# A chunked complex-decay attention with a soft mixture of experts on one core: two chunks' gates joined, masks and results by whole chunks, and a new order of the work

## The chip, the cores and the metric

One core of a Trainium2 chip runs the kernel. The metric is the device time of one execution in microseconds. Other cores of the chip take no part.

## The reference

Two layers follow each other. The first is a linear attention with a complex decay, over 4 batches, 8 heads, 768 steps and a head dimension of 48; the second is a soft mixture of 8 experts with 4 slots each over all 3072 tokens of width 384.

```python
mag = np.sqrt(a_re * a_re + a_im * a_im)
scale = np.minimum(mag, 0.999) / (mag + 1e-06)
for t in range(S):                       # S_re, S_im: 48 x 48 per batch and head
    new_re = ar * S_re - ai * S_im       # ar, ai: a_re, a_im times scale at step t
    new_im = ar * S_im + ai * S_re
    S_re, S_im = new_re + outer(k_t, v_t), new_im
    y_t = q_t @ S_re
logits = x @ phi                         # x: y with the heads side by side
d = softmax(logits, axis=0); c = softmax(logits, axis=1)
slot_out[e] = relu((d.T @ x)[e] @ w1[e]) @ w2[e]
out = c @ slot_out
```

## The kernel before

The sequence is cut into 12 chunks of 64 steps. A chunk j is two tiles (2j and 2j+1), each of 128 partitions: two batches of 64 steps. The decay is used in polar form, so the recurrence inside a chunk becomes products with running sums of logarithms and angles.

The work is a set of small tasks, each a Python generator that issues one step per call, and the string `ORDER` (line 295) names them one by one: a token is a task and, after a colon, its bank of PSUM. `run` (line 883) plays it, and after each token pins the instructions, so that every engine keeps this order. What follows on an engine waits for what stands in front of it there. The tasks:

- `la` loads a group of gates (a_re, a_im), `g` turns them into logarithms of magnitudes by 8 steps (`gates`, line 637), `t` takes the arctangent. A group holds the chunks that `STEPS` (line 47) names: the two tiles of chunk 0 each by itself, chunks 1, 2 and 3 each, then pairs. ScalarE has two sets of tables; `L` and `T` load the one for logarithm and exponential, or that for the angles.
- `p` (line 687) sums angles with TensorE, rounds them to whole turns (VectorE for the first two chunks, then ScalarE) and takes the rest. `v` makes sine and cosine, `e` the exponentials of the summed logarithms; `K` carries the sums into the next chunk.
- `m` multiplies k and q by the exponentials (line 766): the k half by VectorE, the q half by GpSimd. `h` (line 777) multiplies by cosine and sine: the hat, a tile of 1536 columns.
- `xk` and `xq` turn the hats on TensorE and copy the result (line 793); the copy is VectorE's for the tiles and halves of `COPY_V` (line 41: k of tiles 0 to 7, q of tiles 0 to 3), ScalarE's otherwise.
- `c` (line 803), one for each tile, makes scores and masks them; `D` adds to the state; `A` (line 834) gives the results of a chunk, copied for one tile by ScalarE and for the other by VectorE; `F` turns them (copy by ScalarE); `d` applies a decay at chunk 5.
- For each pair of chunks, `l` (line 108) makes the logits and `s` (line 135) the slots' running sums and each token's shares. `s` has the exponential's accumulator give each row's sum `z`, kept in `zrun`, and turns the shares into `ecT`. `me` and `si` merge the slots' sums and give the experts' inputs. `er` (line 271) spreads the turned shares over the experts by products with constant matrices (`C_REP`), in 12 pieces, and masks them.
- `w:` loads one of 32 tiles of expert weights (768 KB, two loads) into a buffer that an earlier task gives back: `wx` are its own, `ar`, `qkt`, `hat` and so on are those of attention. 23 of them stand in the order, each with a wait on the TensorE instruction in front of it in the order and on the third load before it; 9 follow as the first layer of the experts gives buffers back (`used`, line 973).

All loads are issued on SP's queue. After the order come the two expert layers (`hidden`, `experts`) and the mixture, whose results are stored from SP and ScalarE.

Of the kernel before, what the change touches and what calls it, by code (L numbers as in the profile page):

```python
# [11 lines left out]
F32 = mybir.dt.float32  # L12
# [3 lines left out]
ALU = mybir.AluOpType  # L16
# [22 lines left out]
BUF = dict(ar=2, ai=2, gt=1, qkt=3, vt=3, f=3, cs=3, ee=2, hat=3, hTq=3, hTk=2, scT=3, st=3, yT=3, xs=8, wx=4)  # L39
AHEAD, WAHEAD, LATE = 3, 3, 5  # L40
COPY_V = tuple((i, w) for i in range(8) for w in range(2) if i < 4 or w == 0)
PAIRS = ("p", "e", "xk", "xq", "D", "A", "F")
ROUND_V = 4
# [3 lines left out]
STEPS = [(0,), (0,), (1,), (2,), (3,)] + [(j, j + 1) for j in range(4, NCH, 2)]  # L47
# [38 lines left out]
C_REP = C_SEL + P  # L86
C_LOW = C_REP + UB * P
# [3 lines left out]
class _Moe:  # L91


    def __init__(self, nc, pool, work, tr, cst, phi_sb):
        self.nc, self.pool, self.work, self.tr = nc, pool, work, tr
        self.ident, self.sel = cst[:, C_ID:C_BU], cst[0:UR, C_SEL:C_REP]
        self.rep = [cst[0:UR, C_REP + P * j : C_REP + P * (j + 1)] for j in range(UB)]
# [4 lines left out]
        self.z = pool.tile([UR, 1], F32, name="zrun")  # L102
        self.acc = pool.tile([UR, HD], F32, name="acc")
        self.ecT = pool.tile([UR, NU, P], F32, name="ecT")
# [3 lines left out]
    def logits(self, u, yT):  # L108
# [22 lines left out]
        lc = wk.tile([P, UB, NSLOT], F32, name="lc")  # L131
        nc.vector.tensor_tensor(out=lc, in0=lt, in1=mx.broadcast_to([P, UB, NSLOT]), op=ALU.subtract)
        self.mid[u] = (ls, lc)

    def slots(self, u, xs):
        nc, wk, tr = self.nc, self.work, self.tr
        ls, lc = self.mid.pop(u)
        nm = self.nm[u]
        z = wk.tile([UR, 1], F32, name="z")
        self.act(out=ls, in_=ls, func=AF.Exp, bias=nm, accum_out=z)  # L140
# [16 lines left out]
        tp = tr([P, UR + P], "mt")  # L157
        nc.tensor.transpose(out=tp[:, 0:UR], in_=ls, identity=self.ident[0:UR, 0:UR])
# [3 lines left out]
        nc.vector.tensor_copy(out=d, in_=tp[:, 0:UR])  # L162
# [11 lines left out]
    def merge(self):  # L174
# [6 lines left out]
        mrow = wk.tile([1, UB, NSLOT], F32, name="mrow", bufs=1)  # L181
# [114 lines left out]
    L g0 g0 g0 g0 g0 g0 g0 g0 g1 g1 lv1 e0:0 g1 T t0 g1 p0:1 la2 t1 p0 L g1 g1 e0 p1:1 g1 g1 p0 la2 e0 g2 p1 p1 e1:0 g2 T v0  # L296
    g2 la3 m0 v0 la3 g2 t2 v0 p2:2 v1 v1 L g2 lq1 h0 e1 D0:1 e1 p2 g2 g2 lq2 p2 g2 K1 e2:3 g3 g3 xk0:0 la4 g3 la4 T v1 xq0:2
    w:wx g3 m1 h1 L g3 e2 xk0 g3 g3 xq0 e2 g3 g4 K2 c0:0 g4 T v2 v2 g4 m3 D1:2 m2 D0 D1 t3 e3:3 v2 g4 xq1:1 p3:2 c0 xq1 t4 L
    g4 p3 h2 h3 la5 g4 e3 xk1:0 la5 D2:1 p3 p4:2 lq3 D2 xq2:1 g4 g4 g5 m5 e3 lq4 g5 g5 p4 xk1 T v3 v3 K3 xq2 xq3:0 v3 c1:6 p4
    xq3 m4 lv2 xk2:1 v4 xk3:2 g5 e4:0 t5 xk2 h5 xk3 la6 L g5 D3:1 D3 e4 e4 c1 la6 p5:2 g5 p5 h4 g5 c2:7 A0:1 c3:6 g5 g6 A0 K4  # L300
    A0 c2 A0 c3 A0 lq5 e5:0 g6 p5 m7 xq5:3 e5 xk5:1 e5 K5 D5:2 xq5 v4 xk5 F0:0 g6 D5 p6:3 T v5 F0 v4 lv3 v5 m6 p6 A1:1 xk4:2
    xk4 xq4:0 p6 A1 g6 e6:2 c5:6 xq4 h6 c4:7 v5 lv4 c5 c4 m8 A1 xk6:0 A1 A2:3 t6 A1 v6 L g6 xk6 e6 A2 F1:0 A2 la7 e6 F1 A2 h7
    lq6 g6 xq7:1 la7 v6 D4:2 xq7 xk7:0 l0:2 A2 D4 xk7 m9 g6 l0 xq6:2 p7:3 g6 g7 w:wx lv5 D7:1 e7:0 h8 xq6 c6:4 m11 p7 D7 g7 p7
# [43 lines left out]
def _stepwise(ctx, tc, cst, phi_sb, raw, w1, w2, out):  # L347
# [125 lines left out]
    for j in range(UB):  # L473
        for _ in moe.weights(er[j], j, range(UB)):
            pass
        for u in range(UB, NU):
            for _ in moe.weights(er[u][:, j : j + 1], j, [u]):
                pass
# [38 lines left out]
def _polar(ctx, tc, cst, phi_sb, bad, aa, qk, vv, phi, w1, w2, consts, out):  # L517
# [34 lines left out]
    def two():  # L552
        return psum[:, 2 * cur["bank"] : 2 * cur["bank"] + 2]
# [595 lines left out]
```

## Time and profile before

| | us |
|---|---|
| median of 3 runs | 269.25 (268.48 to 270.42) |
| profiled execution, its own time | 265.5 |
| its span, first to last instruction | 263.7 |

Over the span TensorE was busy 80%, VectorE (DVE) 77%, ScalarE (ACT) 73% and GpSimd (POOL) 23%; 55.13 MB were moved, and the mean granted clock of TensorE was 0.949. PEld is TensorE's loading of weights, which runs beside its products. A row of a group gives line, engine, operation, result and operands with their shapes, the number of instructions, then busy time in us and the mean of one in ns, then the idle time before them and what ended it. A row of a timeline gives start and length in us; "x2" are two instructions without a gap between them.

### The profile page before, as it was taken

Reading aid. Unit: us, or ns where it says so; the run is one execution under the profiler, and the core shown is the slowest. Engines: PE = TensorE matmul, PEld = TensorE weight load, DVE = VectorE, ACT = ScalarE, POOL = GpSimd, SP = SyncE. Lnnn points to the kernel's source line nnn. Section 1 sums busy time; section 2 is a strip of 40 time slices with the busy share of each in tenths; the row PEclk is TensorE's granted clock in tenths of the full one; section 3 lists DMA queues with packets and bytes.
Section 4 is the critical chain, followed back from the end, with each engine's and each line's share of the span. In section 5 each row is a group of like instructions: output and inputs, shape, how many; then the busy total and the mean of one; then the engine's idle time right before and its main releaser. Section 6 shows DMA issues by size and latency. Waiting matters only on the chain.

```text
span 263.7 us, 12297 instructions
## 1 busy us (share of the span) xinstructions
PE 211.7 (80%) x5592; PEld 156.8 (59%) x5592; DVE 202.8 (77%) x301; ACT 192.3 (73%) x267; POOL 59.7 (23%) x39
## 2 busy tenths in 40 slices
PE   0626465568799898899999999999989998999740
PEld 0204254245578777678788779678877745268520
DVE  1277999999999999999999889998862668126330
ACT  5998999699899999989989888798743345013320
POOL 0000033463860639040460031250000030000000
PEclk9999659795999999999999999999999999999995
DMA  6763642496321691098612036838998998899994
GB/s 200 277 217 120 221 163 82 160 309 231 121 65 62 224 280 48 5 325 273 188 53 76 6 122 202 245 116 288 307 295 280 276 295 295 280 365 346 376 398 169
DMA packets 21355, 55.13 MB, mean 209 GB/s; under 512 B 2608, under 2 KB 3120, under 8 KB 21296
## 3 DMA queue, kind: packets, MB, share of 16 engines
q1 hardware_dynamic: 20432, 52.70, 60.1%
q10 hardware_dynamic: 864, 1.57, 1.6%
q8 instruction: 46, 0.75, 1.2%
q14 instruction: 13, 0.11, 0.1%
HBM read 49.53 MB, written 4.72 MB: 206 GB/s over the span
## 4 chain that ended last, share of the span: by engine, by line
PE 39%; DVE 31%; DMA 12%; ACT 8%; issue 7%; DVEq 0%; ACTq 0%; SPq 0%
DMA w<-in_w_dram 10%; PE psum L850 7%; PE psum L807 6%; PE psum L796 5%; PE psum L823 5%; DVE hat L780 4%; DVE ar L658 4%; PE psum L842 3%; DVE qkt L773 3%; DVE ar L654 2%; PE psum L676 2%; DVE ar L729 2%; DMA ar<-in_aa_dram 2%; DVE f L698 2%; DVE hTk L801 2%
## 5 line engine op out<-in xcount | busy, mean ns | idle before, releaser
L771 POOL TENSOR_TENSOR qkt<-ee,qkt 128x384 f32<-128x384 f32 x22 | 38.4, 1765 | 61.6 <-ACT ee L721 51.4
L780 DVE TENSOR_TENSOR hat<-qkt,cs 128x1536 f32<-128x1536 f32 x24 | 42.2, 1767 | 3.8 <-PE psum L823 2.1
L796 PE MATMUL psum<-cst,hat 64*96 64x64 f32 x768 | 30.8, 225 | 3.1 <-DVE st L832 1.2
L823 PE MATMUL psum<-vt,hat 64*64 64x48 f32 x1408 | 29.1, 231 | 4.7 <-DVE hTk L801 1.6
L823 PEld LDWEIGHTS psum<-vt,hat 64*64 64x64 f32 x1408 | 26.1, 145 | 9.5 <-DVE hTk L801 2.3
L807 PE MATMUL psum<-hTq,hTk 96*64 96x64 f32 x768 | 28.3, 231 | 4.0 <-DVE hTq L801 3.9
L807 PEld LDWEIGHTS psum<-hTq,hTk 96*64 96x64 f32 x768 | 25.5, 144 | 10.0 <-DVE hTq L801 4.1
L796 PEld LDWEIGHTS psum<-cst,hat 64*96 64x96 f32 x768 | 25.2, 127 | 10.5 <-issue 3.3
L648 POOL TENSOR_TENSOR ai<-ai,gt 128x768 f32<-128x768 f32 x9 | 18.7, 2094 | 56.4 <-ACT gt L642 56.4
L850 PE MATMUL psum<-st,hTq 96*64 96x48 f32 x704 | 25.5, 224 | 0.3 <-issue 0.3
L850 PEld LDWEIGHTS psum<-st,hTq 96*64 96x64 f32 x704 | 22.6, 138 | 2.7 <-issue 1.6
L801 ACT COPY hTq<-psum 96x1024 f32<-96x1024 f32 x20 | 20.0, 1007 | 3.0 <-PE psum L796 2.8
L811 DVE TENSOR_TENSOR scT<-psum,cst 128x512 f32<-128x512 f32 x24 | 16.0, 681 | 7.1 <-PE psum L807 7.1
L830 DVE TENSOR_TENSOR st<-psum,st 96x768 f32<-96x768 f32 x20 | 18.8, 945 | 0.7 <-PE psum L823 0.7
L801 ACT COPY hTk<-psum 96x1024 f32<-96x1024 f32 x16 | 16.0, 1004 | 4.2 <-PE psum L796 3.3
L676 PE MATMUL psum<-ai,cst 64*64 64x384 f32 x88 | 11.9, 602 | 8.1 <-ACT ai L662 3.6
L842 PEld LDWEIGHTS psum<-vt,scT 64*64 64x64 f32 x768 | 12.3, 135 | 4.7 <-DVE ar L729 0.9
L556 ACT ACT_TABLE_LOAD x11 | 14.1, 1283 | 0.9 <-PEq L1129 0.7
L676 PE MATMUL psum<-ar,cst 64*64 64x384 f32 x88 | 9.9, 519 | 5.8 <-DVE ar L729 4.8
L842 PE MATMUL psum<-vt,scT 64*64 64x48 f32 x768 | 13.8, 220 | 0.8 <-DVE ar L729 0.7
L256 PE MATMUL psum<-w,hz 128*32 128x128 f32 x384 | 12.6, 275 | 1.9 <-DMA w<-in_w_dram 1.7
L867 ACT COPY yT<-psum 128x768 f32<-128x768 f32 x12 | 9.6, 798 | 5.5 <-PE psum L864 5.3
(126 smaller groups left out, 405.1 us busy)
## 6 DMA issues: line engine op xcount, KB each, us to landing
w<-in_w_dram SPq DMA_DIRECT2D x64, 384.0 KB
qkt<-in_qk_dram SPq DMA_DIRECT2D x24, 384.0 KB
vt<-in_vv_dram SPq DMA_DIRECT2D x12, 384.0 KB
ar<-in_aa_dram SPq DMA_DIRECT2D x11, 384.0 KB
ai<-in_aa_dram SPq DMA_DIRECT2D x11, 384.0 KB
out_dram<-os SPq DMA_DIRECT2D x12, 256.0 KB
out_dram<-os ACTq DMA_DIRECT2D x6, 256.0 KB
cst<-in_consts_dram SPq DMA_DIRECT2D x1, 386.0 KB
```

The source lines that it names most:

```text
L648: POOL.tensor_tensor(out=i[:, z : z + 2], in0=i[:, z : z + 2], in1=t[:, z : z + 2], op=ALU.mult)
L676: PE.matmul(out=o[C * x : C * (x + 1), y], lhsT=m[r], rhs=g[r, x], start=True, stop=c == 0)
L771: POOL.tensor_tensor(out=t[:, y], in0=ee[j][:, y, w], in1=t[:, y], op=ALU.mult)
L780: DVE.tensor_tensor(out=t, in0=qkt[j][:, y].rearrange("p w (h d) -> p w h d", d=D).unsqueeze(3).broadcast_to([P, 2, H, 2, D]), in1=cs[j][: ...
L796: PE.transpose(out=tp[:, x, h], in_=hat[j, y][half(x), w, h].rearrange("p c d -> p (c d)"), identity=ident[half(x), half(x)])
L801: f(out=t, in_=tp)
L807: PE.matmul(out=sp[half(x), h], lhsT=hT[j, y, 0][:, x, h], rhs=hT[j, y, 1][:, x, h], start=True, stop=True)
L811: DVE.tensor_tensor(out=t, in0=sp, in1=mask[j % 2].unsqueeze(1).broadcast_to([P, H, C]), op=ALU.mult)
L823: PE.matmul(out=db[m : m + 64, x, D * h : D * h + D], lhsT=k_, rhs=vt[j][half(x), y, h, :], start=True, stop=True)
L830: DVE.tensor_tensor(out=t, in0=d, in1=st[j - 1][:, _batches(j, y)], op=ALU.add)
L842: PE.matmul(out=yb[half(x ^ y), y, h], lhsT=scT[j, y][half(x), h], rhs=vt[j][half(x), y, h, :], start=h == 0, stop=h == H - 1 and j == 0)
L850: PE.matmul(out=yb[half(x ^ y), y, h], lhsT=hT[j, y, 1][:, x, h], rhs=st[j - 1][:, _batch(j, y, x), h, :], start=False, stop=h == H - 1)
```

## The change

- Chunks 2 and 3 become one group of gates, as the later pairs are: 8 groups instead of 9.
- `score` takes a chunk: the products of both tiles, in two banks, and then one mask over 1024 columns. `attend` ends with one copy of 768 columns instead of two of 384.
- In the slot steps the accumulator and `zrun` go; the slots' sums are products of the slot weights with a column of ones, one column beside the 384 of `acc`. The turning of the shares goes from there too; shares are kept, and `er`, now 6 tasks, copies them spread out (ScalarE unless said otherwise), turns four 128x128 squares on TensorE and masks them. The constant matrices for spreading go: 512 columns.
- A token can name an engine after `@`. 9 of the q copies, 5 of the k copies, 5 roundings, 2 copies of results, 4 copies of turned results, 2 spreading copies and one gate square are VectorE's; the k products of chunks 1 to 11 (all 11) and one gate product of chunk 0 are GpSimd's. Otherwise a copy is ScalarE's.
- Buffers: 4 of q/k (3), 2 of cosines (3), 2 of masked scores, each for a chunk (3 for a tile), 4 of results for a chunk (8 for a tile).
- The order is a new one, of 678 tokens instead of 733. Its table loads are 19 instead of 21. Of the weights' loads, 4 are for q/k buffers (3) and 2 for cosines (3).

```diff
-BUF = dict(ar=2, ai=2, gt=1, qkt=3, vt=3, f=3, cs=3, ee=2, hat=3, hTq=3, hTk=2, scT=3, st=3, yT=3, xs=8, wx=4)
+BUF = dict(ar=2, ai=2, gt=1, qkt=4, vt=3, f=3, cs=2, ee=2, hat=3, hTq=3, hTk=2, scT=2, st=3, yT=3, xs=4, wx=4)
-STEPS = [(0,), (0,), (1,), (2,), (3,)] + [(j, j + 1) for j in range(4, NCH, 2)]
+STEPS = [(0,), (0,), (1,)] + [(j, j + 1) for j in range(2, NCH, 2)]
...
-        self.act(out=ls, in_=ls, func=AF.Exp, bias=nm, accum_out=z)
+        self.act(out=ls, in_=ls, func=AF.Exp, bias=nm)
...
-        nc.tensor.transpose(out=tp[0:UR, UR : UR + P], in_=lc.rearrange("p a s -> p (a s)"), identity=self.ident)
...
-        nc.vector.tensor_copy(out=self.ecT[:, u, :], in_=tp[0:UR, UR : UR + P])
...
-        sp = tr([UR, HD], "sip")
+        sp = tr([UR, HD + 1], "sip")
         for j in range(UB):
-            nc.tensor.matmul(out=sp[32 * j : 32 * j + 32, :], lhsT=d[:, 32 * j : 32 * j + 32], rhs=xs(j), start=True, stop=True)
+            r = slice(32 * j, 32 * j + 32)
+            nc.tensor.matmul(out=sp[r, HD : HD + 1], lhsT=d[:, r], rhs=self.ones, start=True, stop=True)
+            nc.tensor.matmul(out=sp[r, 0:HD], lhsT=d[:, r], rhs=xs(j), start=True, stop=True)
...
-    def weights(self, out, j, us):
-        ep = self.tr([P, len(us), P], "ep")
-        self.nc.tensor.matmul(out=ep, lhsT=self.rep[j], rhs=self.ecT[:, us[0] : us[-1] + 1, :], start=True, stop=True)
+    def weights(self, out, u):
+        r = self.work.tile([P, 4 * UB, 4, 8], F32, name="rep", bufs=1)
+        v = self.share[:, u].rearrange("p a (g r) -> p (a g) r", g=4).unsqueeze(2).broadcast_to([P, 4 * UB, 4, 8])
+        self.copy("A", r, v)
+        yield "er0"
+        ep = self.tr([P, UB, P], "ep")
+        for a in range(UB):
+            self.nc.tensor.transpose(out=ep[:, a], in_=r[:, 4 * a : 4 * a + 4].rearrange("p g q r -> p (g q r)"), identity=self.ident)
...
+    def copy(engine, out, in_):
+        f = DVE.tensor_copy if on(engine) == "V" else ACT.copy
+        f(out=out, in_=in_)
...
-            DVE.tensor_tensor(out=t, in0=ee[j][:, :, w], in1=t, op=ALU.mult)
+            f = POOL if on("V") == "G" else DVE
+            f.tensor_tensor(out=t, in0=ee[j][:, :, w], in1=t, op=ALU.mult)
...
-    def score(j, y):
-        sp = tr([P, H, C], "sp")
+    def score(j):
+        sp = two()[:, :, 0 : H * C].rearrange("p y (h t) -> p y h t", t=C)
...
-            xs[j, y] = buf("xs", [P, HD])
-            f = DVE.tensor_copy if y else ACT.copy
-            f(out=xs[j, y], in_=yb[:, y].rearrange("p h d -> p (h d)"))
+        yield "a3"
+        xs[j] = buf("xs", [P, 2, HD])
+        copy("A", xs[j], yb.rearrange("p y h d -> p y (h d)"))
```

The first lines of the new order:

```text
L g0 g0 g0 g0 g0 g0 g0 g0 e0:0 g1 g1 T t0 g1@G g1 t1 p0:1 la2 L g1 p0@V g1 la2 e0 p0 e0 g1 g1 g2 g2 m0 T v0 p1:1 lv1 v0 v0
p1@V g2 g2@V t2 p1 L g2 e1:0 la3 h0 g2 la3 e1 e1 p2:2 g2 p2@V g2 lq1 D0:1 xk0:3 g3 K1 g3 g3 e2:0 m1 xk0@V p2 e2 D0 e2 g3
```

## Rows read from the trace of the kernel before

**Rows 1.** Engines by stage: start:end us, length, busy time and instructions, clock, DMA.
```profile
0.00:30.00 30.00, 12.54 (x112) 5.88 (x114) 15.93 (x23) 24.35 (x41) 0.20 (x4) 0.98 0.63 210
30.00:131.00 101.00, 82.72 (x2391) 63.18 (x2390) 99.23 (x113) 95.14 (x117) 42.64 (x23) 0.90 0.52 171
131.00:222.30 91.30, 87.42 (x2605) 70.22 (x2600) 74.03 (x132) 65.47 (x97) 16.88 (x14) 1.00 0.64 202
222.30:263.70 41.40, 28.98 (x508) 17.52 (x508) 13.62 (x37) 7.38 (x14) 0.00 (x0) 0.92 0.88 318
```

**Rows 2.** The chain that ended last, from 222 us: start, length, what.
```profile
222.25 3.38 PE psum L235 x29
...
243.99 7.32 DMA w<-in_w_dram
```

**Rows 3.** SP's timeline: the last run of weight loads.
```profile
176.31 68.01 SPq L568 DMA_DIRECT2D w<-in_w_dram  x54
```

**Rows 4.** Waits of SP's queue, 160 to 252 us: total, times, longest.
```profile
SPq L568 <- DMA w<-in_w_dram: 43.0, 46, 2.5
```

**Rows 5.** Groups of instructions by form: VectorE.
```profile
L780 DVE TENSOR_TENSOR hat<-qkt,cs 128x1536 f32<-128x1536 f32 x24 | 42.2, 1767 | 3.8 <-PE psum L823 2.1 <-ACT cs L710 1.4
...
L811 DVE TENSOR_TENSOR scT<-psum,cst 128x512 f32<-128x512 f32 x24 | 16.0, 681 | 7.1 <-PE psum L807 7.1
...
L773 DVE TENSOR_TENSOR qkt<-ee,qkt 128x768 f32<-128x768 f32 x11 | 13.4, 1216 | 0.0
...
L801 DVE COPY hTk<-psum 96x1024 f32<-96x1024 f32 x8 | 9.7, 1209 | 0.0
...
L654 DVE SCALAR_TENSOR_TENSOR ar<-ar,gt 128x1536 f32<-128x1536 f32 x4 | 7.1, 1769 | 0.0
...
L856 DVE COPY xs<-psum 128x384 f32<-128x384 f32 x12 | 6.6, 552 | 3.0 <-PE psum L850 2.8
...
L654 DVE SCALAR_TENSOR_TENSOR ar<-ar,gt 128x768 f32<-128x768 f32 x3 | 3.7, 1217 | 0.0
...
L694 DVE TENSOR_SCALAR f<-psum 128x768 f32<-128x768 f32 x1 | 1.0, 958 | 0.8 <-PE psum L682 0.8
```

**Rows 6.** Timelines of GpSimd and of VectorE, single instructions.
```profile
37.19 1.92 POOL L648 TENSOR_TENSOR ai<-ai,gt 128x768 f32<-128x768 f32 x1 [36.75 <-ACT gt L642]
...
63.89 6.19 POOL L771 TENSOR_TENSOR qkt<-ee,qkt 128x384 f32<-128x384 f32 x2 [6.70 <-ACT ee L721]
...
37.35 2.58 DVE L773 TENSOR_TENSOR qkt<-ee,qkt 128x768 f32<-128x768 f32 x1
...
77.40 0.94 DVE L773 TENSOR_TENSOR qkt<-ee,qkt 128x768 f32<-128x768 f32 x1
...
130.95 1.75 DVE L780 TENSOR_TENSOR hat<-qkt,cs 128x1536 f32<-128x1536 f32 x1
```

**Rows 7.** Groups of instructions by form: ScalarE.
```profile
L801 ACT COPY hTq<-psum 96x1024 f32<-96x1024 f32 x20 | 20.0, 1007 | 3.0 <-PE psum L796 2.8
...
L556 ACT ACT_TABLE_LOAD x11 | 14.1, 1283 | 0.9 <-PEq L1129 0.7
...
L867 ACT COPY yT<-psum 128x768 f32<-128x768 f32 x12 | 9.6, 798 | 5.5 <-PE psum L864 5.3
...
L652 ACT ACTIVATE gt<-gt 128x1536 f32<-128x1536 f32 x4 | 5.9, 1485 | 0.0
...
L652 ACT ACTIVATE gt<-gt 128x768 f32<-128x768 f32 x3 | 2.5, 842 | 0.0
```

**Rows 8.** Groups of instructions by form: TensorE.
```profile
L274 PE MATMUL psum<-ecT,cst 128*128 128x512 f32 x8 | 4.4, 631 | 0.0
...
L274 PE MATMUL psum<-ecT,cst 128*128 128x128 f32 x16 | 3.3, 311 | 0.2 <-DVE er L269 0.2
...
L119 PE MATMUL psum<-cst,ls 128*128 128x128 f32 x6 | 1.9, 310 | 0.0
...
L167 PEld LDWEIGHTS psum<-xs,d 128*32 128x32 f32 x48 | 1.1, 108 | 0.3
```

More of the change, by code (lines that the diff above doesn't have):

```diff
@@ L101, in __init__ @@
         self.nm, self.mid = {}, {}
-        self.z = pool.tile([UR, 1], F32, name="zrun")
-        self.acc = pool.tile([UR, HD], F32, name="acc")
-        self.ecT = pool.tile([UR, NU, P], F32, name="ecT")
+        self.ones = cst[:, C_ONE : C_ONE + 1]
+        self.acc = pool.tile([UR, HD + 1], F32, name="acc")
+        self.z = self.acc[:, HD : HD + 1]
+        self.copy = lambda engine, out, in_: nc.scalar.copy(out=out, in_=in_)
+        self.share = pool.tile([P, NU, UB, NSLOT], F32, name="share")
         self.wz = pool.tile([UR, 2], F32, name="wz")
@@ L300 @@
[L300 to L303, printed above, removed]
@@ L472, in _stepwise @@
     er = [cp.tile([P, UB, P], F32R, name=f"er{n}") for n in range(NER)]
-    for j in range(UB):
-        for _ in moe.weights(er[j], j, range(UB)):
-            pass
-        for u in range(UB, NU):
-            for _ in moe.weights(er[u][:, j : j + 1], j, [u]):
-                pass
+    for u in range(NU):
+        for _ in moe.weights(er[u], u):
+            pass
     for x in range(NX):
@@ L561, in _polar @@
     moe = _Moe(nc, cp, ys, tr, cst, phi_sb)
+    moe.copy = copy
     ga, gt, qkt, vt = {}, {}, {}, {}
@@ L799, in xpose @@
         hT[j, y, w] = t
-        f = DVE.tensor_copy if (2 * j + y, w) in COPY_V else ACT.copy
-        f(out=t, in_=tp)
-    def score(j, y):
-        sp = tr([P, H, C], "sp")
-        for h in range(H):
-            for x in range(2):
-                PE.matmul(out=sp[half(x), h], lhsT=hT[j, y, 0][:, x, h], rhs=hT[j, y, 1][:, x, h], start=True, stop=True)
-        yield "c1"
-        t = buf("scT", [P, H, C])
-        scT[j, y] = t
-        DVE.tensor_tensor(out=t, in0=sp, in1=mask[j % 2].unsqueeze(1).broadcast_to([P, H, C]), op=ALU.mult)
+        copy("A", t, tp)
+    def score(j):
+        sp = two()[:, :, 0 : H * C].rearrange("p y (h t) -> p y h t", t=C)
+        for y in range(2):
+            for h in range(H):
+                for x in range(2):
+                    PE.matmul(out=sp[half(x), y, h], lhsT=hT[j, y, 0][:, x, h], rhs=hT[j, y, 1][:, x, h], start=True, stop=True)
+            yield f"c{y + 1}"
+        scT[j] = buf("scT", [P, 2, H, C])
+        DVE.tensor_tensor(
+            out=scT[j].rearrange("p y h t -> p (y h) t"),
+            in0=sp.rearrange("p y h t -> p (y h) t"),
+            in1=mask[j % 2].unsqueeze(1).broadcast_to([P, 2 * H, C]),
+            op=ALU.mult,
+        )
     st, yT, xs = {}, {}, {}
@@ L842, in attend @@
                     PE.matmul(
-                        out=yb[half(x ^ y), y, h], lhsT=scT[j, y][half(x), h], rhs=vt[j][half(x), y, h, :], start=h == 0, stop=h == H - 1 and j == 0
+                        out=yb[half(x ^ y), y, h], lhsT=scT[j][half(x), y, h], rhs=vt[j][half(x), y, h, :], start=h == 0, stop=h == H - 1 and j == 0
                     )
         for y in range(2):
-            yield f"a{2 * y + 1}"
+            yield f"a{y + 1}"
             if j:
@@ L948, in zeros @@
     def zeros():
-        late["zs"] = [buf("xs", [P, 3, 4, 32], name=f"zs{hi}") for hi in range(2)]
+        zs = buf("xs", [P, 2, 3, 4, 32], name="zs")
+        late["zs"] = [zs[:, hi] for hi in range(2)]
         late["hz"] = [buf("hTq", [P, 8, 4, 32], name=f"hz{hi}") for hi in range(2)]
@@ L955, in zeros @@
             POOL.memset(t, 0.0)
-    for j in range(UB):
-        at(f"er{j}", lambda j=j: moe.weights(er_tile(j), j, range(UB)))
-    for u in range(UB, NU):
-        for j in range(UB):
-            at(f"er{UB + UB * (u - UB) + j}", lambda u=u, j=j: moe.weights(er_tile(u)[:, j : j + 1], j, [u]))
+    for u in range(NU):
+        at(f"er{u}", lambda u=u: moe.weights(er_tile(u), u))
     at("ze", zeros)
```

115 lines of the change are left out of this document (54 added, 61 removed).

## Prediction

> **What bounds the kernel now.** I read first the busy time of each engine in stages that I cut myself [rows 1]: the table shows whether one engine is full in a stage, and which. Four stages come out. Up to 30 us nothing is full: the gates of chunk 0 go through ScalarE, VectorE and TensorE by turns. From 30 to 131 us VectorE is busy 99.2 of 101 us and ScalarE 95.1; TensorE has 82.7. The two vector engines bound this stage together, so only work taken from both shortens it. From 131 to 222.3 us TensorE is busy 87.4 of 91.3 us, VectorE 74.0 and ScalarE 65.5: TensorE bounds it, and what VectorE saves here is worth little. From 222.3 us the expert layers run, ending at 263.7.
>
> Then the chain that ended last [rows 2]: TensorE starts the first expert layer at 222.25, and the last piece of expert weights lands at 243.99 + 7.32 = 251.3; 12.4 us of small work and stores follow. SP's queue [rows 3] has 54 half loads of weights in one run from 176.31 for 68 us, and its waits [rows 4] say what holds it: in 46 of them, 43.0 us, it is the earlier weight load. So from 176 us the weights come as fast as the transfers go, and the end follows from when this stream can start; but its buffers are those that attention gives back, so the start follows attention. TensorE is itself busy 29.0 us from 222.3 on [rows 1], about the 29 us to the last landing: neither the stream nor attention alone could be moved by more than some 2 us without the other.
>
> **The change part by part.** Rows are means over a group unless I give a start time. I count what each order has done when tile 13 gets its hat (VectorE, at 130.95 us before [rows 6]), the end of the second stage. The counts are from the two order strings, the durations from the rows.
>
> VectorE up to there [rows 5]. The k products of chunks 1 to 6 go to GpSimd: 6 x 1.216 = 7.3 us off by the mean, 6 x 0.94 = 5.6 by one that ran undisturbed [rows 6]; I take 5.6, since the disturbance is counted apart below. Turned copies of q and k: 12 before, 8 after, 4 x 1.209 = 4.8 off. Masks: 12 x 0.681 = 8.2 become 6 of 1024 columns; the nearest row of that length from PSUM is the turned copy, 6 x 1.209 = 7.3, so 0.9 off. Results: 5 x 0.552 = 2.8 become 2 of 768 columns at 0.958, 0.9 off. Two roundings and two copies of yT come over from ScalarE, 4 x 0.958 = 3.8 on. Gates: two groups of 768 columns become one of 1536. Of the two long operations each, 4 x 1.217 go and 2 x 1.769 come, 1.3 off; a product of 768 is added and one of 384 leaves (0.4 on), and one square comes over (1.0 on): 0.1 on. What is merely later in the new order (a carry of a phase, a decay) is about 1 off. Sum: -5.6 - 4.8 - 0.9 - 0.9 + 3.8 + 0.1 - 1 = -9.3 us.
>
> ScalarE up to there [rows 7]. Table loads, 17 to 13: 4 x 1.283 = 5.1 off (over the whole kernel only two go; the others come later, where ScalarE has time). Gates: 12 x 0.842 become 6 x 1.485, 1.2 off, the square 0.8, two accumulator reads 0.4. Two roundings and two copies of yT, at 0.798, 3.2 off. Turned copies, 12 to 17: 5 x 1.007 = 5.0 on. The results, five half ones against three whole ones, about equal. One wave's exponential and rounding stand later in the order, 1.5 off. Sum -7.2 us.
>
> GpSimd [rows 6] gets 11 k products of 768 columns, some 7 of them in this stage. Its operation of that size took 1.92 us at 37.19; it is busy 42.6 of 101 us [rows 1], so there is room for 7 x 1.92 = 13.4 more, and its queue holds nothing but products, gates and, near the end, four clears. But where it works beside VectorE both slow down: the product that VectorE began at 37.35, inside that operation, took 2.58 us, the one at 77.40 took 0.94. That is 1.64 more; for 7 products the bounds are 0 and 11.5 us on VectorE. I take 2, near the low end: the product, whose mean of 1.216 against 0.94 shows it disturbed, is the one that leaves, and the hat, with a mean of 1.767 us for twice the columns [rows 5], shows little. So VectorE has about 7 us less and ScalarE 7.2 less. Both were 94 to 98% full; I take 6.5 us off this stage.
>
> The Trainium skill, SBUF — State Buffer, sections "SBUF: two separate sides" and "Who interferes with whom", speaks against this part: the port pair that GpSimd and VectorE share is an exclusive lock, and a VectorE instruction with two SBUF inputs blocks against a GpSimd instruction that reads SBUF for its whole length. The pair at 37 us [rows 6] agrees: VectorE's product ends 0.82 us after GpSimd's, as if it had begun only then. Elsewhere it is GpSimd that waits: its two halves at 63.89 took 6.19 us. By the rule the gain of this stage could be given back; that is the last case of the third rival.
>
> The head: the second load of constants shrinks by four matrices of 64 KB, and a load of v (384 KB) moves in SP's queue behind that of chunk 1's gates. At the 210 GB/s of the first stage [rows 1] this lets the gates come 262/210 = 1.2 us and 1.9 us sooner, at most 3.1 us together, and worth nothing where ScalarE is busy with chunk 0 until then, as it is for 24.35 of these 30 us. I take 0. The v of chunk 1 is needed only by its state products, some 20 us on.
>
> TensorE after tile 13 [rows 8]. Six turns of shares leave the slot steps, 6 x 0.310 = 1.9 off. The products that spread the shares, 4.4 + 3.3 = 7.7 us, become 24 turns: at most 24 x 0.310 = 7.4, and less when they follow each other; I take 5.5, 2.2 off. The slots' sums add 24 products of one column, two passes each: 48 weight loads x 0.108 = 5.2 us if none hides behind the products of 384 columns beside them, nothing if all do; 2.6. Sum -1.5, bounds +3 and -5. The sums for VectorE and ScalarE that go (slots' z, the accumulator read, the copies of turned shares) lie in stages or queues with room, and so do four new ScalarE copies of 512 columns; if the last shares were late, TensorE would wait for them before the slot inputs, a risk of about 1 us each for the last two. The scores' mask now starts after both tiles' products, so the first tile's result waits for the second's 32 products; that is hidden as long as other TensorE work stands before the results need it, which the order provides, and costs up to 1 us a chunk where not.
>
> The tail: counting TensorE work that is left, the first weight load into a gate buffer is issued about 10 us of it sooner, the fifth some 2 us sooner, and after the last q/k buffer (there are four now, the cosines give back one less) 11 gated tiles are to come where 12 were before, with 2 us less work left. One tile is 68 us / 27 = 2.5 us of stream. So the stream keeps its distance from the expert layers to within 1 us, and what attention saves is passed on.
>
> Total: 6.5 + 1.5 = 8.0 us. The profiled execution took 265.5 us, 3.75 under the median of the runs shown, 269.25. Against its own time 265.5 - 8.0 = 257.5; against the median 261.2.
>
> **The rivals.** First, the stream doesn't follow. If the weights' stream starts no earlier in time than at 176, because the wait on TensorE's place in the order holds the first q/k buffers back, the last piece still lands near 251, and only the 2 us of TensorE's waits there go: 267 to 269. For it: rows 3 and 4 show the stream as the last to end; against it: every load stands at the same or an earlier place of the work.
>
> Second, more than the sum. The merged gates spare waits of one engine for another in the first 80 us, and a denser TensorE would do stage three sooner: with VectorE's 9.3 us in full, TensorE's lower bound of 5 and 1 us of the head, -15: 254. Against it: ScalarE has only 7 to give.
>
> Third, ending on the other side: GpSimd decides when hats start. Each hat needs the k product of its chunk, and with two products per chunk GpSimd has 2 x 1.92 = 3.8 us to do undisturbed, and more where it is blocked: the two halves at 63.89 took 6.19 us [rows 6]. If k products take 3.5 us instead of VectorE's 0.94 and all 11 lie on the path, that is 28 us; with half of them covered, 14, less the 8: 275. It decides from the point where the product, once the chunk's exponentials are done, takes longer than VectorE's other work before the hat, which in the new order, summed with these durations, is 2 to 9 us. For it: the 6.19 us. Against it: GpSimd was idle for more than half of the second stage and four fifths of the third, so it starts at once. With blocking of VectorE alone, the 11 x 1.92 = 21 us more of GpSimd meet operations with two SBUF inputs (hats 42.2, long gate operations 7.1, of 202.8 us) for a quarter to a third of their time: some 6 us are given back and the time is 267, within 1%.
>
> **How the numbers follow.** Forecast (256 to 266) 0.60; more than the sum (250 to 256) 0.12; the stream or the blocking takes the gain (266.5 to 272) 0.16; GpSimd decides (over 272) 0.12. A difference of 1%, 2.7 us, is about what a measurement of this kernel can tell from none: faster 0.72, same 0.16, slower 0.12. The range 253 to 271 leaves out the lower half of the second case and the slow one, 0.18 with some of the third; the likeliest case's own range is 256 to 266.
>
> **What would show it.** Right: table loads 19, VectorE's product rows down to those of chunk 0, 22 products with GpSimd plus 11 wide ones; VectorE some 190 us busy and ScalarE 183; tile 13's hat at about 124.5, the first expert product at about 214, the last weights at about 243. Wrong: the hat of tile 13 not earlier than 128 with TensorE or VectorE waiting for GpSimd's products (GpSimd the releaser in the waits); or the expert layer earlier but the last weights still at 250.

## The result, and the profile after

| | before | changed |
|---|---|---|
| median of 20 runs each, us | 268.50 (265.15 to 273.63) | 264.36 (261.12 to 269.02) |
| profiled execution, its own time (span), us | 265.5 (263.7) | 264.75 (263.0) |
| ratio, 95% interval | | 0.9863 [0.9824, 0.9901] |

The change makes the kernel faster by 4.1 us in the medians, half of the 8.0 forecast. The ratio is taken over the faster executions of each kernel, so it lies a little nearer to 1 than the ratio of the medians (0.985). The two profiled executions show only 0.7 us of the gain: that of before lies 3.0 us under its median, that of the changed kernel 0.4 above. So I read single traces for where time sits, and take sizes from medians and from several traces together.

The page's busy times of the changed kernel's engines over its span, and TensorE's granted clock in 40 slices:

```profile
PE 208.5 (79%) x5634; PEld 156.6 (60%) x5634; DVE 197.9 (75%) x260; ACT 185.1 (70%) x237; POOL 73.9 (28%) x50
...
PEclk9986667999799999996899999999999999999975
```

Table loads are 19 (10 and 9), as in the diff. ScalarE at 185.1 us is near the 183 forecast. VectorE at 197.9 is not: 190 were expected. GpSimd has 73.9 us. The windows by stage, as in [rows 1] (columns: PE, PEld, DVE, ACT and POOL busy, granted clock, DMA share, GB/s):

```profile
0.00:30.00 30.00, 11.50 (x112) 5.46 (x112) 16.59 (x22) 25.13 (x38) 2.80 (x6) 0.85 0.62 201
30.00:131.00 101.00, 84.62 (x2435) 65.12 (x2435) 95.38 (x94) 90.56 (x103) 46.71 (x30) 0.89 0.57 182
131.00:219.80 88.80, 82.68 (x2595) 68.30 (x2588) 71.12 (x111) 61.78 (x84) 24.38 (x16) 1.00 0.61 191
219.80:263.00 43.20, 29.69 (x508) 17.73 (x508) 14.79 (x37) 7.58 (x15) 0.00 (x0) 0.88 0.86 312
```

In the second stage VectorE still works 95.4 of 101 us, ScalarE 90.6, and that stage ends nearly as before: tile 13's hat stands at 130.10 us, where it stood at 130.95 [rows 6]; 124.5 was forecast. The first expert product comes at 219.77 instead of 222.25 [rows 2], and the last stage has become 1.8 us longer.

Part of why VectorE is no emptier is in its groups by form. The mask of 1024 columns (L816) is as long as assumed (1216 ns), but of the two long gate operations (L658, L662) the first, which took 1769 ns [rows 5, there L654], now takes 2401 (2010 and 2180 in two later traces), and the second 1910:

```profile
L786 DVE TENSOR_TENSOR hat<-qkt,cs 128x1536 f32<-128x1536 f32 x24 | 43.4, 1817 | 0.0
...
L816 DVE TENSOR_TENSOR scT<-psum,cst 128x1024 f32<-128x1024 f32 x12 | 14.6, 1216 | 7.0 <-PE psum L813 7.0
...
L658 DVE SCALAR_TENSOR_TENSOR ar<-ar,gt 128x1536 f32<-128x1536 f32 x5 | 12.0, 2401 | 0.1
...
L662 DVE SCALAR_TENSOR_TENSOR ar<-ar,gt 128x1536 f32<-128x1536 f32 x5 | 9.6, 1910 | 0.0
```

The timelines of the changed kernel show when. Rows of VectorE, GpSimd and TensorE (start, length; in brackets the idle time before and what ended it):

```profile
113.91 3.40 DVE L658 SCALAR_TENSOR_TENSOR ar<-ar,gt 128x1536 f32<-128x1536 f32 x1
117.23 0.94 DVE L702 SCALAR_TENSOR_TENSOR f<-f,psum 128x768 f32<-128x768 f32 x1
...
121.49 2.56 DVE L662 SCALAR_TENSOR_TENSOR ar<-ar,gt 128x1536 f32<-128x1536 f32 x1
...
113.87 1.82 POOL L779 TENSOR_TENSOR qkt<-ee,qkt 128x768 f32<-128x768 f32 x1
116.68 2.31 POOL L779 TENSOR_TENSOR qkt<-ee,qkt 128x768 f32<-128x768 f32 x1 [0.99 <-ACT ee L728]
118.95 3.48 POOL L776 TENSOR_TENSOR qkt<-ee,qkt 128x384 f32<-128x384 f32 x2
...
118.23 0.65 PE L802 MATMUL psum<-cst,hat 64*96 64x64 f32 x16 [1.32 <-DVE f L702]
...
124.24 3.17 PE L813 MATMUL psum<-hTq,hTk 96*64 96x64 f32 x64
```

GpSimd begins a k product at 113.87, VectorE its gate operation 0.04 us later. GpSimd ends at 115.69; VectorE ends at 117.31, 1.62 us after that, about one undisturbed length (1.75): the times fit an operation that stood still until GpSimd was through. The rounded angles (L702), queued behind, come late, and TensorE waits 1.32 us for them. Between 120 and 125 us its granted clock is 0.50, its 1.2 GHz level, and 64 products take 3.17 us; that the wait brought the clock down is not shown. At 121.49 VectorE is held up again, beside the second of two q products.

This is what the Trainium skill says (SBUF — State Buffer, section "Who interferes with whom"): a VectorE instruction with two SBUF inputs and a GpSimd instruction that reads SBUF need one shared port pair, and the later one waits for the whole of the other. The trace agrees (3.40 us = 1.78 + 1.62). The rounding at 117.23, with one input from PSUM, ran its undisturbed 0.94 us inside GpSimd's next product (116.68 to 118.99), as that section says too.

The last stage, from the chain that ended last; SP's last run of loads; and, in TensorE's timeline, the last products that waited for weights:

```profile
219.77 9.65 PE psum L227 x88
...
232.28 4.72 DMA w<-in_w_dram
...
237.02 6.52 DMA w<-in_w_dram
...
243.60 7.32 DMA out_dram<-os
```

```profile
182.34 60.09 SPq L570 DMA_DIRECT2D w<-in_w_dram  x46
```

```profile
250.32 0.63 PE L248 MATMUL psum<-w,hz 128*32 128x128 f32 x12 [0.74 <-DMA w<-in_w_dram]
```

After 12.5 us of the first expert layer the chain is transfers. The weights' last run begins at 182.34 (176.31 in [rows 3], but with eight halves more in it) and its issuing ends at 242.4, where [rows 3] end at 244.3. The last weights land at 250.3, where they landed at 251.3 before [rows 2]; about 243 was forecast. So the stream gained 1 to 2 us. In two later traces of the changed kernel the chain has no weight transfer in this stage, so this reading holds for one trace.

### The profile page after: what moved, and what is told of

The parts are those of the page before. It is cut to its first block, busy times and chain, and to the rows that moved or that the text cites. A ratio compares the mean times of both kernels' runs of the same rounds, so it can differ in the third digit from the quotient of the medians.

```text
span 263.0 us, 12332 instructions
## 1 busy us (share of the span) xinstructions
PE 208.5 (79%) x5634; PEld 156.6 (60%) x5634; DVE 197.9 (75%) x260; ACT 185.1 (70%) x237; POOL 73.9 (28%) x50
## 4 chain that ended last, share of the span: by engine, by line
PE 45%; DVE 20%; ACT 16%; DMA 9%; issue 7%; ACTq 0%; DVEq 0%; SPq 0%
PE psum L813 7%; PE psum L802 6%; PE psum L860 6%; PE psum L833 6%; DMA w<-in_w_dram 4%; DVE hat L786 4%; PE psum L227 4%; DVE ar L658 4%; PE psum L852 3%; PE psum L680 3%; DMA out_dram<-os 3%; DMA ar<-in_aa_dram 2%; PE psum L873 2%; ACT gt L644 2%; ACT L560 2%
## 5 line engine op out<-in xcount | busy, mean ns | idle before, releaser
L776 POOL TENSOR_TENSOR qkt<-ee,qkt 128x384 f32<-128x384 f32 x22 | 32.9, 1515 | 29.7 <-issue 18.5
L779 POOL TENSOR_TENSOR qkt<-ee,qkt 128x768 f32<-128x768 f32 x11 | 23.3, 2121 | 38.4 <-ACT ee L728 19.8
L833 PE MATMUL psum<-vt,hat 64*64 64x48 f32 x1408 | 27.9, 233 | 4.4 <-DVE hat L786 1.8
L833 PEld LDWEIGHTS psum<-vt,hat 64*64 64x64 f32 x1408 | 25.5, 147 | 7.7 <-DVE hat L786 2.0
L649 POOL TENSOR_TENSOR ai<-ai,gt 128x768 f32<-128x768 f32 (+1 forms) x9 | 15.4, 1727 | 34.4 <-ACT gt L644 24.2
L551 ACT COPY hTk<-psum 96x1024 f32<-96x1024 f32 x19 | 18.9, 1006 | 3.6 <-PE psum L802 3.6
L816 DVE TENSOR_TENSOR scT<-psum,cst 128x1024 f32<-128x1024 f32 x12 | 14.6, 1216 | 7.0 <-PE psum L813 7.0
L551 ACT COPY hTq<-psum 96x1024 f32<-96x1024 f32 x15 | 15.0, 1005 | 5.7 <-PE psum L860 3.2
L852 PE MATMUL psum<-vt,scT 64*64 64x48 f32 x768 | 15.0, 221 | 2.2 <-issue 2.2
L658 DVE SCALAR_TENSOR_TENSOR ar<-ar,gt 128x1536 f32<-128x1536 f32 (+2 forms) x8 | 14.1, 1760 | 3.0 <-ACT gt L656 2.9
L551 ACT COPY xs<-psum 128x768 f32<-128x768 f32 x10 | 8.0, 799 | 10.3 <-PE psum L860 6.9
```

The source lines that it names most:

```text
L551: f(out=out, in_=in_)
L658: DVE.scalar_tensor_tensor(out=r, in0=r, scalar=2.0, in1=t, op0=ALU.mult, op1=ALU.add)
L776: f.tensor_tensor(out=t[:, y], in0=ee[j][:, y, w], in1=t[:, y], op=ALU.mult)
L779: f.tensor_tensor(out=t, in0=ee[j][:, :, w], in1=t, op=ALU.mult)
L833: PE.matmul(out=db[m : m + 64, x, D * h : D * h + D], lhsT=k_, rhs=vt[j][half(x), y, h, :], start=True, stop=True)
L852: PE.matmul(out=yb[half(x ^ y), y, h], lhsT=scT[j][half(x), y, h], rhs=vt[j][half(x), y, h, :], start=h == 0, stop=h == H - 1 and j == 0)
```

## The experiments

The theory after reading the two traces: the work that left VectorE did leave, but GpSimd's k products hold VectorE up by almost as much as they relieve it. The rivals: the stage is no longer VectorE's but a chain's through the hand-written order; the gain is there but the stream of weights doesn't pass it on. Each kernel was measured beside the kernel before, and the ratios are to that.

**The changed kernel once more.**

> The changed kernel as it is, once more, as the base of this group and for a second trace. Both theories: ratio to the kernel before 0.980 to 0.992; tile 13's hat between 127 and 132 us and the first expert product between 217 and 221 us, as in the first trace. If the second trace has them 3 us or more elsewhere, single traces of this kernel don't carry differences of that size.

Measured: 265.67 us, ratio 0.9919 [0.9847, 0.9991]; tile 13's hat at 129.51, but the first expert product at 225.58, 5.8 us later than in the first trace and outside the range expected, with a slower clock in the slices before it. The execution profiled took 268.39 us, 2.7 above the median. The second stage repeats from trace to trace; the third doesn't, to some 6 us.

**The k products back on VectorE** (11 tokens lose their `@G`):

```
-    m4@G D3:3 ... m6@G ... m22@G
+    m4 D3:3 ... m6 ... m22
```

> The changed kernel with the 11 products of k back on VectorE, nothing else moved. Theory 'given back' (GpSimd's products block VectorE's instructions with two SBUF operands for as long as VectorE gains): within 1.5 us of the changed kernel, ratio to before 0.981 to 0.992; VectorE's stretched gate and hat operations fall back to 1.75 us. Rival 'the move carries the gain': 4 to 8 us slower than the changed kernel, ratio 1.00 to 1.015.

Measured: 266.46 us, 0.998 [0.9938, 1.0021], hat 13 at 129.87. The gate operations are back at their length, and the seven products of this stage cost 7.9 us on VectorE. Groups by form up to 129.87 us:

```profile
L779 DVE TENSOR_TENSOR qkt<-ee,qkt 128x768 f32<-128x768 f32 x7 | 7.9, 1132 | 0.0
...
L658 DVE SCALAR_TENSOR_TENSOR ar<-ar,gt 128x1536 f32<-128x1536 f32 x4 | 7.0, 1749 | 0.1
```

So the stage takes as long with these 7.9 us on VectorE. The ratios differ by 0.6% (0.998 against 0.992) and the medians by 0.8 us; the kernel before differs from itself by 0.7% in the last run below, so no gain of the move is shown. Why the stage is no longer, with VectorE busy 115.0 us up to the hat where the changed kernel has 112.5 in the mean, isn't settled; TensorE's granted clock up to there is 0.96, and 0.88 to 0.93 in the changed kernel's traces. In the forecast 3.6 us of the 8.0 hung on it.

**No k products** for chunks 1 to 11; this kernel leaves that factor out of the computation:

```
-            f = POOL if on("V") == "G" else DVE
-            f.tensor_tensor(out=t, in0=ee[j][:, :, w], in1=t, op=ALU.mult)
+            pass
```

> The changed kernel with the products of k by the exponentials left out for chunks 1 to 11: no engine does them. Theory 'given back': 3 to 6 us faster than the changed kernel, ratio 0.964 to 0.975, since VectorE loses some 5 us of blocking up to tile 13. Rival 'the order's own waits set this stage, GpSimd costs nothing there': within 1 us of the changed kernel, ratio 0.982 to 0.990.

Measured: 259.97 us, 0.9732 [0.9628, 0.9836], hat 13 at 124.76. With the products gone and not moved, the stage is 5.3 us shorter than the mean of the changed kernel's three traces (130.06) and the end 5.7 us earlier than in the repeat above, as the theory had it. On GpSimd the products still cost the stage those 5 us, 3.8 of them as VectorE's busy time up to the hat (108.7 us here, 112.5 in the mean of the three); how far the rest is TensorE's, whose granted clock is higher here too (0.95), isn't separated. The rows of all engines up to that hat, in the kernel before, in the repeat and here (columns as above):

```profile
0.00:130.95 130.95, 95.21 (x2494) 69.01 (x2496) 115.11 (x134) 119.44 (x157) 42.80 (x26) 0.92 0.54 180
...
0.00:129.51 129.51, 95.39 (x2495) 69.39 (x2497) 112.42 (x114) 114.52 (x139) 47.59 (x34) 0.92 0.59 189
...
0.00:124.76 124.76, 92.34 (x2502) 65.79 (x2504) 108.65 (x114) 113.92 (x139) 33.74 (x27) 0.95 0.61 194
```

**The kernel before with only its k products on GpSimd**:

```
-            DVE.tensor_tensor(out=t, in0=ee[j][:, :, w], in1=t, op=ALU.mult)
+            POOL.tensor_tensor(out=t, in0=ee[j][:, :, w], in1=t, op=ALU.mult)
```

> The kernel before with only its 11 products of k moved to GpSimd, in its own order. Theory 'given back': within 1% of the kernel before, ratio 0.992 to 1.010. Rival 'the move carries the gain': 4 us or more faster, ratio 0.970 to 0.985. A third way, hats that wait for GpSimd: slower, 1.01 to 1.03, with GpSimd the releaser of the hats.

Measured: 273.32 us, 1.015 [0.9979, 1.0321], hat 13 at 135.86. The interval holds 1, so that the kernel is slower is likely and not shown. Here two hats do wait for GpSimd, as in the third rival of the prediction; VectorE's waits from 30 to 130 us (total, times, longest):

```profile
DVE hat L780 <- POOL qkt L773: 1.9, 2, 1.4
```

In the changed kernel no such wait appears in the same view: no hat is held up by a late product.

**Each k product twice on GpSimd**, the first into a tile that nobody reads:

```
+            if f is POOL:
+                twice = io.tile([P, 2, 352], mybir.dt.bfloat16, name="twice", bufs=1)
+                f.tensor_tensor(out=twice, in0=ee[j][:, :, w, 0:352], in1=t[:, :, 0:352], op=ALU.mult)
             f.tensor_tensor(out=t, in0=ee[j][:, :, w], in1=t, op=ALU.mult)
```

> The changed kernel, in which GpSimd does each of its 11 k products twice: the first into a tile that nobody reads (704 of 768 columns, bfloat16), then the real one. That is some 18 us more for GpSimd (74 to 92 us busy) and no work for VectorE. Theory (while GpSimd works, VectorE's own instructions stand still for part of the time; the 5.1 us of slower VectorE instructions up to tile 13 come from some 50 us of GpSimd): VectorE's busy time rises by 3 to 5 us over 197.9, hat of tile 13 at 132 to 134 us, ratio 0.995 to 1.01. Rival (GpSimd at 28 per cent has room, its products are beside VectorE and cost it nothing): VectorE's busy time within 1 us of 198, hat of tile 13 within 1 us of 130, ratio 0.985 to 0.993.

Measured: 269.29 us, 1.0066 [0.9976, 1.0156], hat 13 at 132.17. The page of this kernel:

```profile
PE 212.8 (79%) x5634; PEld 158.0 (59%) x5634; DVE 206.0 (77%) x260; ACT 185.1 (69%) x237; POOL 102.6 (38%) x61
```

VectorE has 206.0 us where the changed kernel's three traces have 197.9, 200.0 and 201.9, with the same 260 instructions. GpSimd's 26 to 29 us more (18 were expected) put 4 to 8 on VectorE, and no hat waits for GpSimd. The hat and the ratio are as the theory had them, VectorE's rise is larger; the rival falls.

**The copies of the turned tiles on their engines of before** (in the changed order; the `@V` of `xk` and `xq` go as well):

```
-        copy("A", t, tp)
+        copy("V" if i_ < 8 and (i_ < 4 or w == 0) else "A", t, tp)
```

> The changed kernel with the copies of the turned tiles put back on the engines that they had before: VectorE copies k of tiles 0 to 7 and q of tiles 0 to 3, ScalarE the rest. Up to the hat of tile 13 that is 12 copies on VectorE where the changed kernel has 8 (four more at 1.22 us = +4.9 us), behind it none where it has 6. Theory (VectorE still decides the stage up to tile 13; what it was spared by GpSimd came back as slower instructions and waits): hat of tile 13 at 133 to 134.5 us where the changed kernel has 129.5 to 130.1, ratio to the kernel before 0.995 to 1.005. Rival (the stage is no longer VectorE's, a chain through TensorE and its banks sets it): hat of tile 13 within 1 us of 130, VectorE's waits shorter by some 4 us, ratio 0.985 to 0.993.

Measured: 289.22 us, 1.0781 [1.064, 1.0923], hat 13 at 152.35. Both expectations missed by far. VectorE's busy time up to that hat is 113.0 us, as in the changed kernel (111.1 to 113.9): the 22 us are all waiting, with TensorE's granted clock at 0.82. Where it starts, in TensorE's and ScalarE's timelines of this kernel:

```profile
48.16 1.09 PE L803 MATMUL psum<-cst,hat 64*96 64x64 f32 x16 [3.56 <-DVE hTq L551]
```

```profile
52.83 0.81 ACT L725 ACTIVATE ee<-psum 128x768 f32<-128x768 f32 x1 [6.99 <-PE psum L680]
```

TensorE waits for a turned q that VectorE copies behind a hat, and ScalarE, in its own order, waits 6.99 us for TensorE. That made a new theory, tested with a single copy.

**One copy moved**, that of tile 0's q:

```
- ... h2 xq0 xq3:1
+ ... h2 xq0@V xq3:1
```

> The changed kernel with one copy moved: that of the turned q of tile 0 goes from ScalarE (where two such copies ran as one row of 1.92 us at 40.86 us) to VectorE, at its place in the order, behind the hat that starts at 44.13 us. By a sum of durations this is 1.22 us more for VectorE and some 0.95 us less for ScalarE. Theory (in orders written out by hand a copy's place decides and not its length; the 289 us with all copies on their engines of before came from copies that stood behind a hat while TensorE, and through it ScalarE, waited): the first scores (L813 at 43.68 us) start at 47 to 49 us, the fifth hat (56.2 to 56.6 us) at 60 us or later, the hat of tile 13 at 133 us or later, the end 3 us or more later, ratio 1.0 or more. Rival (the sum): the fifth hat within 1.5 us of 56.5, hat of tile 13 at 131 us at most, ratio 0.985 to 0.996.

Measured: 269.03 us, 1.0014 [0.9974, 1.0054], against 0.9895 [0.9835, 0.9955] for the changed kernel measured beside it; the first scores at 48.22 us (42.94 there), the fifth hat at 62.45 (56.62), hat 13 at 134.83 (130.57). The timelines of this kernel:

```profile
45.93 1.22 DVE L551 COPY hTq<-psum 96x1024 f32<-96x1024 f32 x1
...
47.20 1.09 PE L802 MATMUL psum<-cst,hat 64*96 64x64 f32 x16 [4.90 <-DVE hTq L551]
...
51.75 0.81 ACT L725 ACTIVATE ee<-psum 128x768 f32<-128x768 f32 x1 [6.84 <-PE psum L680]
```

and, in the changed kernel's trace taken beside it, the two copies on ScalarE:

```profile
40.97 1.92 ACT L551 COPY hTq<-psum 96x1024 f32<-96x1024 f32 x2
```

A copy of 1.22 us, at 45.93 instead of 41, costs 4 to 6 us in that stage and 1.2% at the end; the two intervals don't meet. The theory holds for this copy; that the 289 us are many such places is inferred from it.

**The changed kernel a third time**, as the base of that comparison:

> The changed kernel itself, as the base for the other two on this chip: ratio 0.982 to 0.995, hat of tile 13 at 129 to 131 us, the 46 halves of weights in 59.5 to 61 us.

Measured: 266.68 us, 0.9895 [0.9835, 0.9955], hat 13 at 130.57, 46 halves in 59.24 us.

**The stream without TensorE's places.** In the changed kernel each load also waits for the TensorE instruction ahead of it in the order:

```
-    ... WAHEAD if gated else LATE, gated)
+    ... WAHEAD if gated else LATE, gated and x < 4)
```

> The changed kernel, in which the weights' loads from the fifth tile on don't wait for the TensorE instruction that stands ahead of them in the order; they still wait for a free tile and for the load three before. Theory (in the last stage the stream of weights decides: in the changed kernel SP waits 18 us for TensorE between 160 and 182 us and some 7 us between 182 and 200, with a DMA share of 0.53 to 0.77 between 180 and 200 where the kernel before had 0.90 to 0.95, so that a gain of 2.5 us at the first expert product is 0.7 us at the end): the DMA share between 180 and 200 is 0.85 or more, the last weights land at 246 to 248 us instead of 250.2, the end is 1.5 to 3 us earlier, ratio 0.975 to 0.984. Rival (the tiles come free no sooner, or the loads of weights delay v of the last chunks by as much): the last weights within 1 us of 250, ratio 0.985 to 0.993.

Measured: 267.04 us, 0.9902 [0.9734, 1.0071]: no verdict. Its trace has the 46 halves in 58.86 us and no wait for weights in the last stage's chain, which is TensorE's own:

```profile
221.67 9.65 PE psum L227 x88
...
234.28 3.24 PE psum L248 x112
...
240.01 3.06 PE psum L248 x103
```

From the first expert product to the end it has 39.6 us; the changed kernel 43.2, 40.9 and 41.8. But the execution profiled took 263.16 us, 3.9 under the median, and in the second and third trace of the changed kernel the chain of the last stage holds no wait for weights either. So what the waits for weights cost the tail stays open, at most 1 to 4 us. The DMA share at 180 to 190 us stayed under 0.8, against the expectation.

**Five loads ahead instead of three**, with TensorE's places, and then without:

```
-AHEAD, WAHEAD, LATE = 3, 3, 5
+AHEAD, WAHEAD, LATE = 3, 5, 5
```

> The changed kernel, in which a load of weights waits for the load five before it in place of three (for TensorE's place in the order as before). Theory (the stream of the last stage is held by its start and by the DMA engines' share of 0.9 and more, not by how many halves are under way): the 46 halves that took 60.1 us in the changed kernel take 58.5 to 60, the end within 1 us, ratio 0.983 to 0.993. Rival (three in flight are too few): 46 halves in 54 to 57 us, last weights at 246 us, the end 2 to 3 us earlier, ratio 0.975 to 0.982.

Measured: 268.87 us, 0.9947 [0.9792, 1.0102], 46 halves in 61.88 us: no faster, so the rival falls, though ratio and stream lie a little above the theory's ranges too. From the first expert product to the end this trace has 39.8 us, with TensorE's places kept, so the 39.6 above can't be put down to their absence.

> The changed kernel, in which the weights' loads from the fifth tile on wait neither for TensorE's place in the order nor for the load three before, but for that five before. Each alone gave: without TensorE's place, 46 halves in 58.9 us from 181.5 us and 39.6 us from the first expert product to the end, where the changed kernel has 60.1 us from 182.3 us and 43.2 us; with five ahead, 61.9 us. Theory (the stream ends the last stage; what holds it is the places in the order and, behind those, the DMA engines): as without TensorE's place alone, the end 39.5 to 41 us behind the first expert product with no wait for weights of 4 us or more in the chain, 1 to 3 us under the changed kernel in the same call, ratio 0.975 to 0.985. Rival (the last stage is TensorE's own, the stream hidden): within 1 us of the changed kernel in the same call.

Measured: 278.8 us, 1.0405 [1.0339, 1.047]. Both expectations missed. SP's timeline, one window and one of SP's waits (160 to 190 us) of this kernel:

```profile
189.08 0.33 SPq L570 DMA_DIRECT2D vt<-in_vv_dram  x1
```

```profile
180.00:190.00 10.00, 10.00 (x209) 8.26 (x203) 4.46 (x6) 2.56 (x4) 0.00 (x0) 0.50 0.02 3
```

```profile
SPq L570 <- PE psum L833: 12.1, 1, 12.1
```

The last load of v is issued at 189.08; it stood at 180.64 in the changed kernel measured beside it. TensorE is at its 1.2 GHz level between 180 and 190 us (granted clock 0.50) while almost nothing is moved. SP's waits between 160 and 190 us are led by one of 12.1 us for TensorE's state products (L833), the last of which end at 189.02, where the load of v goes out. So in this trace a late TensorE holds up the load; what made TensorE late first stays open.

**The kernel before, a second trace.**

> The kernel before itself, for a second trace of it: its profiled execution (265.5 us) was 3 us under its median (268.5), while that of the changed kernel (264.75) was at its median (264.36), so the two traces differ by 0.7 us where the medians differ by 4.1. The changed kernel's six traces with the same head have the hat of tile 13 at 129.3 to 131.7 us. Theory A (the difference of the medians lies up to tile 13, the one trace of before was quick there): hat of tile 13 at 132.5 us or later, first expert product at 224 us or later. Theory B (up to tile 13 the two kernels are level within 1 us, the rest lies behind): hat of tile 13 at 130 to 132 us, first expert product at 224 us or later, or the time from there to the end above 42 us. Ratio to itself 0.995 to 1.005.

Measured: 268.53 us; tile 13's hat at 134.07, the first expert product at 226.91. Against itself the ratio is 0.993 [0.9882, 0.9978], so a difference of 0.7% between two kernels shouldn't be read here. It speaks for theory A; with two traces of before 3 us apart at tile 13, how much of the median's 4.1 us lies up to tile 13 stays open to some 2 us.

## Why the prediction was half right

The direction and the range held (264.4 in 253 to 271, and in the likeliest case's 256 to 266); the size was off by half. The two later comparisons give less than the first: 3.0 and 1.9 us in the medians. Of the prediction's own signs, the counts of loads and products came true; but the hat of tile 13 came no earlier than 128 us, and in the first trace the expert layer came earlier with the last weights still at 250, which it had named as signs of being wrong. GpSimd as the releaser in the waits, the other half of the first sign, did not appear: its share shows as longer instructions. By the prediction's own steps:

**VectorE up to tile 13.** From VectorE's timeline each instruction up to that hat is compared with its form's undisturbed length (the one that a tenth of its instances stay under, over all the traces); what it took beyond that is called disturbance:

| us, up to tile 13's hat | work, undisturbed | disturbance | busy | ScalarE busy | hat at |
|---|---|---|---|---|---|
| before, two traces | 118.2 | 5.2, 5.3 | 115.1, 115.3 | 119.4, 119.7 | 130.95, 134.07 |
| changed, three traces | 108.5 | 9.3, 10.7, 12.2 | 111.1, 112.4, 113.9 | 114.8, 114.5, 114.4 | 130.10, 129.51, 130.57 |
| no k products | 108.5 | 7.0 | 108.7 | 113.9 | 124.76 |
| k products on VectorE | 115.1 | 7.4 | 115.0 | 116.6 | 129.87 |
| k products twice | 108.5 | 13.9 | 115.6 | 114.6 | 132.17 |
| one copy moved | 109.7 | 8.2 | 111.4 | 113.7 | 134.83 |

The count of work was right: 118.2 - 108.5 = 9.7 us, where the prediction's sum has 9.3. One term was read from a disturbed mean: the long gate operations of 768 columns are 0.95 us undisturbed, not 1.217, so joining the gates saves 0.3 us there and not 1.3; somewhat more work than assumed stands later in the order and makes up for it. ScalarE's rows sum to 6.9 us less (7.2 forecast), and its busy time fell by 5.0.

**The step that failed is "I take 2, near the low end"**, the disturbance of VectorE by GpSimd. It rose from 5.2 to a mean of 10.7: 5.5 us. A smaller term was left out altogether, on both engines: rows of one engine overlap (117.23 begins 0.08 us before the 113.91 row ends), on VectorE by 8.2 us in the sum over the 134 instructions before and 6.7 over the 114 after, so a sum of row lengths counts 1.5 us of the saving that busy time doesn't show. VectorE's busy time up to there fell by 9.7 - 5.5 - 1.5 = 2.7 us, where "about 7" was forecast; the hat, in the mean of the traces, by 2.5. With the 1.5 of the third stage that would be 4.2, near the first comparison's 4.1; but the 1.5 isn't shown, and the later comparisons have less, so the agreement is partly luck. The prediction had the right mechanism. As the last case of its third rival it had nearly the right price too ("some 6 us are given back"), though that was meant for all 11 products over the whole kernel and gave 267 us.

In its working it took the product that leaves as the victim and the hat as proof of calm. The victims in the changed kernel, in the mean of three traces, were the merged gate operations (3.1 us, and 1.0 before; the new order places them where GpSimd begins its product), the absolute value (L712, 2.7 and 1.5) and the hats themselves (2.0 and 0.1). The split differs from trace to trace.

The runs agree on the cause. Without the k products the disturbance is 7.0 and the stage 5.3 us shorter; with them on VectorE it is 7.4, and the stage no longer than with them on GpSimd; with each done twice it is 13.9, and the hat comes 2 us later. So 3.7 of the 5.5 us go with the moved products; the rest came with the new order and what else it places beside GpSimd. Hats that wait for GpSimd (the rival's 275) are seen in the old order, for 1.9 us, and not in the new one.

**The copies between VectorE and ScalarE.** Counted as 4.8 us less for VectorE. The sum can't price them: with the old engines the stage is 22 us longer at the same busy time of VectorE, and one copy of 1.22 us costs 4 us. The new engines belong to the new order.

**TensorE's third stage, -1.5.** The small terms came out in the changed kernel's rows as a larger gain in busy time, 4.1 us: the turned shares are gone (1.9), the 24 spreading turns take 3.9 us (5.5 assumed) instead of 7.7, the 48 ones-products 1.6 us busy (2.6):

```profile
L271 PE MATMUL psum<-cst,rep 128*128 128x128 f32 x24 | 3.9, 284 | 0.0
...
L158 PE MATMUL psum<-cst,d 128*32 128x1 f32 x48 | 1.6, 181 | 0.0
```

But from tile 13's hat to the first expert product the traces have 91.3 and 92.8 us before, 89.7, 96.1 and 90.3 after: the stage's own scatter hides a gain of this size. The 1.5 us are not shown.

**The tail.** From the first expert product to the end: 41.5 and 40.1 before, 43.2, 40.9 and 41.8 after; 43.3 without k products, where attention ends 4.6 us sooner than in the third changed trace and the kernel 3.1 us. From the kernel without k products to the latest of the changed traces it is 9.3 us and 6.9. So the end follows attention by two thirds to three quarters over these traces, not to within 1 us; the first rival (267 to 269) was too strong, and not empty.

**The head** cost nothing: the fourth hat stands at 44.13 us, and at some 45 before, though TensorE has one wait of 7.8 us between 30 and 60 us for the joint gates' arctangent (L666).

## What to carry to other kernels

Moving work from a full VectorE to an idle GpSimd relieves VectorE only by what GpSimd doesn't take back: look which instructions of VectorE with SBUF operands will run beside it, and price them before counting the relief (here some 0.5 us for each product of 1.8 us and more that GpSimd did, against 0.94 saved). Such a price shows as longer instructions, and not among the waits. In an order written by hand, an instruction's place in its engine's queue can cost several times its length, so a sum of busy times prices work that is removed, and not work that changes engines. Rows overlap, so check a sum of lengths against busy time. Trace a kernel more than once before placing a difference of 2 us in a stage.

## What the runs showed of the hardware

A shared port shows as whole lengths: 3.40 us for an operation of 1.75 that began 0.04 us into GpSimd's 1.82, and for an operation with a PSUM operand nothing (0.94 us). One operation with a single SBUF input is held up too: the absolute value of 768 integers (L712), 0.55 us alone, took 2.05 us at 85.22 in the kernel with each product twice, where GpSimd worked from 85.16 for 1.68 us. The same section of the Trainium skill names tensor_scalar among the instructions whose 2-port modes take the pair; the trace agrees:

```profile
85.22 2.05 DVE L712 TENSOR_SCALAR cs<-f 128x768 int32<-128x768 int32 x1
...
85.16 1.68 POOL L781 TENSOR_TENSOR twice<-ee,qkt 128x704 bf16<-128x704 f32 x1
```

And some waits of TensorE were followed by its 1.2 GHz level, which adds to what the wait cost: in the kernel with one copy moved, 32 score products took 1.97 us behind a wait of 4.90 us (granted clock 0.63 in the mean of 40 to 50 us), and 1.15 us in the changed kernel's trace taken beside it (1.00).
